# Two products accumulated in one PSUM bank, half of the activation read from it, and the last group's quarters stored one by one

## The chip, the cores and the metric

The kernel runs on one core of one Trainium2 chip. The core has five engines with queues of their own: TensorE (PE, matmuls; PEld is its weight load), VectorE (DVE), ScalarE (ACT), GpSimd (POOL) and SyncE (SP, which here only issues transfers). PE writes its results into PSUM, a small memory of eight banks of 512 fp32 columns on 128 partitions; DVE and ACT read PSUM, POOL does not. The metric is the device time in microseconds of one execution; lower is better.

## The reference

The input x has the shape 8 x 3008 x 256 (batch, sequence, features). First comes a two-dimensional Fourier transform over sequence and features of which the real part is kept; then each of the 24064 resulting rows goes through a two-layer network with 2048 hidden units and the activation h * sigmoid(1.702 h).

```python
X = np.fft.fft(x, axis=1)
X = np.fft.fft(X, axis=2)
attn = X.real.astype(np.float32).reshape(8 * 3008, 256)

h = attn @ w_in                              # 256 -> 2048
g = h * (1.0 / (1.0 + np.exp(-1.702 * h)))
out = (g @ w_out).astype(np.float32)         # 2048 -> 256
```

All is fp32.

## The kernel before, in words

**The transform.** 3008 = 94 x 32. For each batch element `fold1` (POOL) and `mix1` (PE, with a copy by ACT) do the part over 94, `spill` and `fill` turn the layout through DRAM, and `stage2` (PE, L277) does the part over 32. Its result is the tile pq, which holds two planes: P (`pq[:, 0]`) and Q (`pq[:, 1]`). The transform over the features is not carried out as such: it is folded into the first layer's weights (`fold_w`), which gives two weight tiles, `wcs[0]` for P and `wcs[1]` for Q. The first batch element has a faster way through the same stages (`mix_first`, `shuffle_first`), while the weights are still being loaded and rounded to fewer bits (`bounds`, `round_in`, `round_out`, `finish_in`, `finish_out`: lines L314 to L336, on ACT, POOL and DVE).

**The rows come in pairs.** Sequence rows s and -s have hidden values that are the sum and the difference of the product with P and the product with Q (with a correction of the Nyquist column, the tile nb times the scalar af2). So one pass over P and Q gives the hidden values of two rows.

**The steps.** Main work is a list of 384 steps (b, blk, hh, p): 8 batch elements, 3 blocks each, 2 halves hh of up to 256 columns (256, 241 or 240), and 8 pairs p of hidden chunks. The eight steps of one (b, blk, hh) form a group. In step t the code issues, one after the other:

- `hidden(t)`: four matmuls on PE. Two fill the bank pa with the product with P, two the bank pb with the product with Q (L397). ACT copies pa to the SBUF tile v (L401).
- `product(t - 3)`: the second layer for the step of three steps ago (L464). For the first group these are eight matmuls, for all later ones seven, in Strassen's scheme (the seven-product way to multiply 2 x 2 blocks), with sums of weights in wt and sums of activations in s. They add up over the eight steps of a group in the four PSUM tiles po0 to po3, which the pool holds once. At the group's end ACT copies po0's first half to u0 (L469).
- `activate(t - 1)` on ACT (L426), then the first two sums of `sums(t - 1)` on POOL (L438, L439), the other two of step t - 2 on DVE (L441, L442).
- `rows(t)` on DVE: h = v + pb (L411), then dif = nb * af2 - pb (L414, twice), then the mirrored rows h = v + dif (L421).
- `combine(t - 3)` on DVE, at a group's end only: the seven additions that undo Strassen's scheme (L493), each of which reads po, then two transposes (L495), then `store`, which issues 32 transfers (L512) for a half-block: on SP, or for the last group on SP and ACT by turns.
- what the schedule adds with `at(t, ...)`: `fold1` and `mix1` of the next batch element, `stage2`, the rounding of weights in the first steps.

Within an engine the order is that in which the code issues. Across engines only the data decide: an instruction waits for what it reads, and for those who still read what it overwrites. The pool `psm` has four PSUM banks for pa, pb and all transform stages, the pool `pso` the four banks of po.

```python
    for t in range(n + LAG):
        if t < n:
            hidden(t)
        if t >= LAG:
            product(t - LAG)
```

The functions that the diff touches, and what calls them:

Of the kernel before, what the change touches and what calls it, by code (L numbers as in the profile page):

```python
# [24 lines left out]
F32 = mybir.dt.float32  # L25
U32 = mybir.dt.uint32
ALU = mybir.AluOpType
ACTF = mybir.ActivationFunctionType
# [10 lines left out]
LAG = 3  # L39
# [6 lines left out]
def free(ap, offset, *dims):  # L46
    return bass.AP(ap.tensor, ap.offset + offset, [list(ap.ap[0])] + [list(d) for d in dims])
# [45 lines left out]
def kernel(ctx: ExitStack, tc, x, w_in, w_out, tab1, tab2, out):  # L93
    nc = tc.nc
    B, S, D = x.shape
# [3 lines left out]
    NBLK = NG // 4  # L99
# [7 lines left out]
    sp = ctx.enter_context(tc.tile_pool(name="sp", bufs=2, space=SB))  # L107
    op = ctx.enter_context(tc.tile_pool(name="op", bufs=2, space=SB))
# [10 lines left out]
    m2 = small[:, 0:256].rearrange("p (c n) -> p c n", c=2)  # L119
    rot = small[:, 256:384]  # L120
    cd = small[:, 384:384 + 4 * H].rearrange("p (i c d) -> p i c d", i=2, c=2)
    wcs = [const.tile([128, DF], F32, tag=f"wcs{i}", name=f"wcs{i}") for i in range(2)]
# [6 lines left out]
    def mat(w, j, rows=NA, n=96):  # L129
        return w[0:rows, j * 96:j * 96 + n]  # L130

    def bank(name):
        return psm.tile([128, 512], F32, tag="mm", name=name)
# [205 lines left out]
    last = {}  # L339
# [38 lines left out]
    steps = [(b, blk, hh, p) for b in range(B) for blk in range(NBLK) for hh in range(2) for p in range(NP)]  # L378
    vb, ht, st, pot, ot = {}, {}, {}, {}, {}

    def width(blk, hh):

        return 241 if (blk, hh) == (0, 1) else 240 if (blk, hh) == (NBLK - 1, 1) else 256

    def two(ap, n):
        return free(ap, 0, [256, 2], [1, n])

    def hidden(t):

        b, blk, hh, p = steps[t]  # L390
        n = width(blk, hh)
        pq, ks = pqt[b, blk], slice(hh * 256, hh * 256 + n)
        pa, pb = bank("pa"), bank("pb")
        for ps, cs in ((pa, 0), (pb, 1)):
            for i in range(2):
                f = 2 * p + i
                nc.tensor.matmul(ps[:, i * 256:i * 256 + n], lhsT=wcs[cs][:, f * 128:(f + 1) * 128],  # L397
                                 rhs=pq[:, cs, ks], start=True, stop=True)
        v = sp.tile([128, 512], F32, tag="v", name="v")

        nc.scalar.copy(two(v[:], n), two(pa[:], n))  # L401
        vb[t] = v, pb

    def rows(t):
        b, blk, hh, p = steps[t]
        n = width(blk, hh)
        nb, ks = nbt[b, blk], slice(hh * 256, hh * 256 + n)
        v, pb = vb.pop(t)
        h = ht[t] = hp.tile([128, 2, 2, 256], F32, tag="h", name="h")
        dif = sp.tile([128, 512], F32, tag="dif", name="dif")  # L410
        nc.vector.tensor_tensor(two(h[:], n), two(v[:], n), two(pb[:], n), op=ALU.add)  # L411
        for i in range(2):
            f = 2 * p + i
            nc.vector.scalar_tensor_tensor(dif[:, i * 256:i * 256 + n], nb[:, ks], af2[:, f:f + 1],  # L414
                                           pb[:, i * 256:i * 256 + n], op0=ALU.mult, op1=ALU.subtract)

        full, rest = divmod(n, NB)
        for at, blocks, m in ((0, full, NB), (full * NB, 1, rest)):
            if m:
                ins = [free(x[:], at, [256, 2], [NB, blocks], [1, m]) for x in (v, dif)]  # L420
                nc.vector.tensor_tensor(free(h[:], 512 + at + m - 1, [256, 2], [NB, blocks], [-1, m]), *ins, op=ALU.add)  # L421

    def activate(t):
        b, blk, hh, p = steps[t]
        g = free(ht[t][:], 0, [256, 4], [1, width(blk, hh)])
        nc.scalar.activation(g, g, ACTF.Gelu_apprx_sigmoid)  # L426

    def sums(t, eng):

# [11 lines left out]
            eng.tensor_tensor(s2, s1, a11, op=ALU.subtract)  # L441
            eng.tensor_tensor(s4, a12, s2, op=ALU.subtract)  # L442

    def product(t):

        b, blk, hh, p = steps[t]
        n = width(blk, hh)
        if p == 0:
            for q in range(4):
                pot[q] = pso.tile([128, 2, 256], F32, tag=f"o{q}", name=f"po{q}")  # L450
        h = ht.pop(t)
        if t < NP:

            plan = [(half, dh, wo[:, p, 2 * f + dh, :], h[:, half, f, :n], f)
                    for half in range(2) for dh in range(2) for f in range(2)]
        else:
            s = st.pop(t)
            plan = ((0, 0, wo[:, p, 0, :], h[:, 0, 0, :n], 0), (0, 1, wt[:, p, 1, :], s[:, 1, :n], 0),
                    (1, 0, wo[:, p, 2, :], h[:, 0, 1, :n], 0), (1, 1, wt[:, p, 2, :], s[:, 2, :n], 0),
                    (2, 0, wt[:, p, 0, :], s[:, 0, :n], 0), (2, 1, wo[:, p, 3, :], s[:, 3, :n], 0),  # L460
                    (3, 0, wt[:, p, 3, :], h[:, 1, 1, :n], 0))

        for q, i, lhs, rhs, f in plan:
            nc.tensor.matmul(pot[q][:, i, :n], lhsT=lhs, rhs=rhs, start=(p == 0 and i == 0 and f == 0),  # L464
                             stop=(p == NP - 1), skip_group_check=True)
        if p < NP - 1 or t < NP:
            return
        c1 = pot["c"] = op.tile([128, 256], F32, tag="u0", bufs=1, name="u0")
        nc.scalar.copy(c1[:, :n], pot[0][:, 0, :n])  # L469

    def combine(t):

        b, blk, hh, p = steps[t]
        if p < NP - 1:
            return
        n = width(blk, hh)
        o = op.tile([128, 4, 256], F32, tag="os", name="os")
        if t < NP:
            for half in range(2):
                nc.vector.transpose(o[:, 2 * half:2 * half + 2, :].rearrange("p i n -> p (i n)"),  # L480
                                    pot[half][:].rearrange("p i n -> p (i n)"))
        else:
            c = cv.tile([128, 4, 256], F32, tag="m", name="c")
            if n < 256:
                nc.gpsimd.memset(c[:, :, n:], 0.0)
            (_, m6), (m2, m7), (m5, m3), (m4, _) = ((pot[q][:, 0, :n], pot[q][:, 1, :n]) for q in range(4))
            u2, u3, u4 = (op.tile([128, 256], F32, tag=f"u{q}", bufs=1, name=f"u{q}")[:, :n] for q in (1, 2, 3))
            c1 = pot["c"][:, :n]
            c11, c12, c21, c22 = (c[:, q, :n] for q in range(4))
            for out_, i0, i1, how in ((u2, c1, m6, ALU.add), (c11, c1, m2, ALU.add), (u3, u2, m7, ALU.add),  # L490
                                      (u4, u2, m5, ALU.add), (c12, u4, m3, ALU.add), (c22, u3, m5, ALU.add),
                                      (c21, u3, m4, ALU.subtract)):
                nc.vector.tensor_tensor(out_, i0, i1, op=how)  # L493
            for half in range(2):
                nc.vector.transpose(*(x[:, 2 * half:2 * half + 2, :].rearrange("p i n -> p (i n)") for x in (o, c)))  # L495
        store(b, blk, hh, o, n)

    def store(b, blk, hh, o, n):

        a = 4 * blk + 2 * hh  # L500
        last = (b, blk, hh) == (B - 1, NBLK - 1, 1)
        for half in range(2):
            sign = -1 if half else 1
            row, step = sign * kp(0, a) % NA, sign * (kp(1, a) - kp(0, a))
            for i in range(8):
                dh, q = divmod(i, 4)
                src = o[32 * q:32 * q + 32, 2 * half + dh, :]
                eng = nc.scalar if last and i % 2 else nc.sync

                def put(row, k2s, places, src):  # L510
                    dst = view(out, (b * S + row) * D + 32 * i, [NA * D, k2s], [step * D, places], [1, 32])
                    eng.dma_start(out=dst, in_=src.rearrange("p (n c) -> p n c", c=32))  # L512

                full, rest = divmod(n, NB)
                put(row, NB, full, src[:, 0:full * NB])
                if rest:

                    k1, lo = kp(NU - 1, a + 1), rest - 16
                    k2, p0, p1 = (16 + lo, lo, 16) if half else (0, 0, rest)
                    put(k1 + NA * k2, p1 - p0, 1, src[p0:p1, 224:256])  # L520
# [57 lines left out]
    n = len(steps)  # L578
# [47 lines left out]

    for t in range(n + LAG):
        if t < n:
            hidden(t)
        if t >= LAG:  # L630
            product(t - LAG)
        if t in early:
            fold_w(early[t])
            nyquist_weights(early[t])

        if 0 < t <= n:
            activate(t - 1)
            sums(t - 1, nc.gpsimd)
        sums(t - 2, nc.vector)
        if t < n:  # L640
            rows(t)
        if t >= LAG:
            combine(t - LAG)
        for fn, args in extra.get(t, ()):
            fn(*args)
# [28 lines left out]
```

## Time and profile before

| | |
|---|---|
| time, median of 3 runs | 1973.1 us (1971.18 to 1975.15) |
| span of the profiled run | 1969.6 us |
| PE busy | 1938.4 us (98%) |
| DVE busy | 1555.3 us (79%) |
| POOL busy | 793.8 us (40%) |
| ACT busy | 695.8 us (35%) |
| L411, h = v + pb, DVE, 384 times | 675 ns each |
| L426, activation, ACT, 384 times | 1044 ns each |
| L401, copy of pa, ACT, 384 times | 577 ns each |
| matmuls L397 and L464 | 375 or 376 ns a record, two records a matmul |

An fp32 matmul shows as two records. Records overlap: a matmul of 256 columns takes 375 ns by its record, but two records start every 0.43 us. An engine's "busy" share is an average over the whole run; what matters is whether it is busy in the stretch in question, and who waits for it. In the lines of the order of time the columns are: start in us, duration in us (of all the instructions merged in the line), engine, line, operation, output <- inputs, shapes, how many, and in brackets the idle time before it and who ended it. In the table by stretch they are: stretch, its length, then busy time and number of instructions of PE, PEld, DVE, ACT and POOL, granted PE clock, share of the transfer engines, GB/s.

### The profile page before, as it was taken

What the parts mean: (1) busy time and instruction counts of PE and PEld (TensorE: products, weight loads), DVE (VectorE), ACT (ScalarE), POOL (GpSimd) and SP (SyncE); (2) the same over time, 40 slices, a digit from 0 to 9 for tenths busy, and PEclk for the clock granted to TensorE, in tenths of its full rate; (3) what the DMA queues carried; (4) which work ended last, traced back from release to release, by engine and by line L of the source; (5) the groups of instructions that cost most, each with busy time, mean ns of one, the idle gap of its engine ahead of it and who ended that gap; (6) DMA issues with size and microseconds to landing.
All of it is one profiled execution on the core that took longest, in us unless ns stands there. A gap on an engine that the chain in (4) does not pass through costs nothing.

```text
span 1969.6 us, 26665 instructions
## 1 busy us (share of the span) xinstructions
PE 1938.4 (98%) x9290; PEld 1724.3 (88%) x9290; DVE 1555.3 (79%) x2893; ACT 695.8 (35%) x970; POOL 793.8 (40%) x1065
## 2 busy tenths in 40 slices
PE   6999999999999999999999999999999999999997
PEld 4698899988989889888899888998899988989886
DVE  4778788888788777887788878887878888778776
ACT  2633333333333333333333333333333333333332
POOL 5476323543245332463325622255323543223232
PEclk8999999999999999999999999999999999999999
DMA  6720441216202252123422252221611213202201
GB/s 197 204 46 11 82 85 15 46 43 121 17 11 48 52 111 17 16 51 57 98 20 45 37 98 42 24 47 43 113 22 14 17 44 58 17 11 23 21 11 22
DMA packets 241837, 101.31 MB, mean 51 GB/s; under 512 B 209651, under 2 KB 232561, under 8 KB 239713
## 3 DMA queue, kind: packets, MB, share of 16 engines
q1 hardware_dynamic: 238965, 97.42, 28.7%
q10 hardware_dynamic: 2736, 2.18, 0.4%
q8 instruction: 73, 1.20, 0.3%
q14 instruction: 63, 0.52, 0.1%
HBM read 56.28 MB, written 45.76 MB: 52 GB/s over the span
## 4 chain that ended last, share of the span: by engine, by line
PE 96%; ACT 1%; DMA 1%; DVE 1%; issue 0%; POOL 0%; DVEq 0%; SPq 0%; POOLq 0%
PE po L464 58%; PE pa L397 16%; PE pb L397 16%; PE ps L189 2%; PE ps L277 2%; DMA raw<-in_moe_w_in_dram 0%; DMA t<-xt 0%; PE ps L241 0%; PE psw L366 0%; PE ps L240 0%; ACT g L314 0%; ACT r L322 0%; ACT r L321 0%; PE psa L372 0%; PE ps L192 0%
## 5 line engine op out<-in xcount | busy, mean ns | idle before, releaser
L438 POOL TENSOR_TENSOR s<-h 128x256 f32<-128x256 f32 (+2 forms) x376 | 273.8, 728 | 1098.2 <-ACT h L426 1026.6
L464 PE MATMUL po<-s,wt 128*128 128x256 f32 (+2 forms) x2256 | 600.0, 375 | 0.0
L401 ACT COPY v<-pa 128x512 f32<-128x512 f32 (+2 forms) x384 | 221.6, 577 | 893.1 <-PE pa L397 893.1
L411 DVE TENSOR_TENSOR h<-v,pb 128x512 f32<-128x512 f32 (+2 forms) x384 | 259.3, 675 | 336.6 <-PE pb L397 329.1
L464 PEld LDWEIGHTS po<-s,wt 128*128 128x128 f32 x2256 | 428.8, 190 | 48.3
L464 PE MATMUL po<-h,wo 128*128 128x256 f32 (+2 forms) x1632 | 469.9, 375 | 0.0
L421 DVE TENSOR_TENSOR h<-v,dif 128x512 f32<-128x512 f32 (+3 forms) x512 | 436.1, 871 | 13.2
L426 ACT ACTIVATE h<-h 128x1024 f32<-128x1024 f32 (+2 forms) x384 | 400.8, 1044 | 11.1 <-DVE h L421 11.1
L397 PE MATMUL pa<-pq,wcs 128*128 128x256 f32 (+2 forms) x1536 | 389.0, 376 | 0.0
L397 PE MATMUL pb<-pq,wcs 128*128 128x256 f32 (+2 forms) x1536 | 387.7, 375 | 0.0
L464 PEld LDWEIGHTS po<-h,wo 128*128 128x128 f32 x1632 | 310.1, 190 | 35.4
L414 DVE SCALAR_TENSOR_TENSOR dif<-nb,af,pb 128x256 f32<-128x256 f32 (+2 forms) x768 | 328.3, 469 | 0.0
L397 PEld LDWEIGHTS pb<-pq,wcs 128*128 128x128 f32 x1536 | 291.9, 190 | 33.0
L397 PEld LDWEIGHTS pa<-pq,wcs 128*128 128x128 f32 x1536 | 287.3, 190 | 33.0 <-issue 0.8
L439 POOL TENSOR_TENSOR s<-h 128x256 f32<-128x256 f32 (+2 forms) x376 | 277.6, 738 | 0.0
L442 DVE TENSOR_TENSOR s<-h,s 128x256 f32<-128x256 f32 (+2 forms) x376 | 211.3, 562 | 13.0
L464 PE MATMUL po<-h,wt 128*128 128x256 f32 (+2 forms) x752 | 220.5, 375 | 0.0
L464 PE MATMUL po<-s,wo 128*128 128x256 f32 (+2 forms) x752 | 220.5, 375 | 0.0
L441 DVE TENSOR_TENSOR s<-s,h 128x256 f32<-128x256 f32 (+2 forms) x376 | 175.3, 466 | 1.2 <-POOL s L438 1.2
L464 PEld LDWEIGHTS po<-s,wo 128*128 128x128 f32 x752 | 142.9, 190 | 16.1
L464 PEld LDWEIGHTS po<-h,wt 128*128 128x128 f32 x752 | 142.9, 190 | 16.1
L195 ACT COPY xt<-ps 96x512 f32<-96x512 f32 x56 | 32.5, 581 | 161.0 <-PE ps L189 151.2
(76 smaller groups left out, 878.0 us busy)
## 6 DMA issues: line engine op xcount, KB each, us to landing
out_dram<-os SPq DMA_DIRECT2D x512, 32.0 KB
Td<-xt SPq DMA_DIRECT2D x7, 1536.0 KB
t<-Td SPq DMA_DIRECT2D x7, 1536.0 KB
Xr<-in_x_dram SPq DMA_DIRECT2D x7, 1410.0 KB
xt<-in_x_dram SPq DMA_DIRECT2D x7, 1280.0 KB
xt<-Xr SPq DMA_DIRECT2D x7, 1200.0 KB
out_dram<-os SPq DMA_DIRECT2D x248, 28.0 KB
nb<-pq SPq DMA_DIRECT2D x23, 256.0 KB
```

Of the source, the lines that this page charges most:

```text
L189: nc.tensor.matmul(ps[0:96, o:o + D], lhsT=mat(w1, jj), rhs=t[:, NB - jj, :], start=True, stop=True)
L397: nc.tensor.matmul(ps[:, i * 256:i * 256 + n], lhsT=wcs[cs][:, f * 128:(f + 1) * 128], rhs=pq[:, cs, ks], start=True, stop=True)
L401: nc.scalar.copy(two(v[:], n), two(pa[:], n))
L411: nc.vector.tensor_tensor(two(h[:], n), two(v[:], n), two(pb[:], n), op=ALU.add)
L414: nc.vector.scalar_tensor_tensor(dif[:, i * 256:i * 256 + n], nb[:, ks], af2[:, f:f + 1], pb[:, i * 256:i * 256 + n], op0=ALU.mult, op1=AL ...
L421: nc.vector.tensor_tensor(free(h[:], 512 + at + m - 1, [256, 2], [NB, blocks], [-1, m]), *ins, op=ALU.add)
L426: nc.scalar.activation(g, g, ACTF.Gelu_apprx_sigmoid)
L438: eng.tensor_tensor(s1, a21, a22, op=ALU.add)
L439: eng.tensor_tensor(s3, a11, a21, op=ALU.subtract)
L441: eng.tensor_tensor(s2, s1, a11, op=ALU.subtract)
L442: eng.tensor_tensor(s4, a12, s2, op=ALU.subtract)
L464: nc.tensor.matmul(pot[q][:, i, :n], lhsT=lhs, rhs=rhs, start=(p == 0 and i == 0 and f == 0), stop=(p == NP - 1), skip_group_check=True)
```

## The change

There are three parts.

1. `hidden` is split in two. `hidden(t, 0)` computes the product with P into a bank pab, and ACT copies it to v, doubled (scale 2). `hidden(t, 1)` then adds the product with Q onto the same bank. The bank now holds P + Q, the hidden value of the first row, so L411 goes away; the mirrored row needs P - Q, which is 2P - (P + Q), so L414 and L421 do it with the doubled v and the same bank. `product` is split too, four matmuls and then the rest, and the order of issue becomes P, four matmuls of the older step, Q, the other three. This gives ACT's copy time to finish before PE writes the bank again.
2. `activate` works in two pieces: one on the mirrored rows in SBUF, one that reads P + Q from the bank and writes h.
3. In `combine` the additions are put in another order, and for the very last group each quarter of the result is transposed and stored as soon as it is there, its transfers alternating between SP and ACT.

The purpose is to take an addition per step off DVE, to use one PSUM bank a step and not two, and to begin the last stores sooner.

```diff
-    def hidden(t):
+    def hidden(t, cs):
...
-        pa, pb = bank("pa"), bank("pb")
-        for ps, cs in ((pa, 0), (pb, 1)):
-            for i in range(2):
-                f = 2 * p + i
-                nc.tensor.matmul(ps[:, i * 256:i * 256 + n], lhsT=wcs[cs][:, f * 128:(f + 1) * 128],
-                                 rhs=pq[:, cs, ks], start=True, stop=True)
-        v = sp.tile([128, 512], F32, tag="v", name="v")
-
-        nc.scalar.copy(two(v[:], n), two(pa[:], n))
-        vb[t] = v, pb
+        if cs == 0:
+            vb[t] = sp.tile([128, 512], F32, tag="v", name="v"), bank("pab")
+        v, ps = vb[t]
+        for i in range(2):
+            f = 2 * p + i
+            nc.tensor.matmul(ps[:, i * 256:i * 256 + n], lhsT=wcs[cs][:, f * 128:(f + 1) * 128], rhs=pq[:, cs, ks],
+                             start=(cs == 0 and i == 0), stop=(cs == 1), skip_group_check=True)
+        if cs == 0:
+
+            nc.scalar.activation(two(v[:], n), two(ps[:], n), ACTF.Copy, scale=2.0)
...
-        nc.vector.tensor_tensor(two(h[:], n), two(v[:], n), two(pb[:], n), op=ALU.add)
...
     def activate(t):
...
-        g = free(ht[t][:], 0, [256, 4], [1, width(blk, hh)])
+        n = width(blk, hh)
+        v, ps = vb.pop(t)
+        g = free(ht[t][:], 512, [256, 2], [1, n])
         nc.scalar.activation(g, g, ACTF.Gelu_apprx_sigmoid)
+        nc.scalar.activation(free(ht[t][:], 0, [256, 2], [1, n]), two(ps[:], n), ACTF.Gelu_apprx_sigmoid)
...
-        for q, i, lhs, rhs, f in plan:
+        for q, i, lhs, rhs, f in plan[4 * part:4 * part + 4]:
...
-            for out_, i0, i1, how in ((u2, c1, m6, ALU.add), (c11, c1, m2, ALU.add), (u3, u2, m7, ALU.add),
-                                      (u4, u2, m5, ALU.add), (c12, u4, m3, ALU.add), (c22, u3, m5, ALU.add),
+            for out_, i0, i1, how in ((c11, c1, m2, ALU.add), (u2, c1, m6, ALU.add), (u4, u2, m5, ALU.add),
+                                      (c12, u4, m3, ALU.add), (u3, u2, m7, ALU.add), (c22, u3, m5, ALU.add),
                                       (c21, u3, m4, ALU.subtract)):
                 nc.vector.tensor_tensor(out_, i0, i1, op=how)
+                if t < len(steps) - 1:
+                    continue
+                for q, done in enumerate((c11, c12, c21, c22)):
+                    if out_ is done:
+                        nc.vector.transpose(o[:, q, :], c[:, q, :])
+                        store(b, blk, hh, o, n, (q,))
...
-            hidden(t)
+            hidden(t, 0)
         if t >= LAG:
-            product(t - LAG)
+            product(t - LAG, 0)
+        if t < n:
+            hidden(t, 1)
+        if t >= LAG:
+            product(t - LAG, 1)
```

`rows` reads the bank under the name ps and no longer as pb; `store` takes the quarters to be stored as a further argument.

More of the change, by code (lines that the diff above doesn't have):

```diff
@@ L407, in rows @@
         nb, ks = nbt[b, blk], slice(hh * 256, hh * 256 + n)
-        v, pb = vb.pop(t)
+        v, ps = vb[t]
         h = ht[t] = hp.tile([128, 2, 2, 256], F32, tag="h", name="h")
         dif = sp.tile([128, 512], F32, tag="dif", name="dif")
-        nc.vector.tensor_tensor(two(h[:], n), two(v[:], n), two(pb[:], n), op=ALU.add)
         for i in range(2):
@@ L414, in rows @@
             nc.vector.scalar_tensor_tensor(dif[:, i * 256:i * 256 + n], nb[:, ks], af2[:, f:f + 1],
-                                           pb[:, i * 256:i * 256 + n], op0=ALU.mult, op1=ALU.subtract)
+                                           ps[:, i * 256:i * 256 + n], op0=ALU.mult, op1=ALU.subtract)
         full, rest = divmod(n, NB)
@@ L442, in sums, with product @@
             eng.tensor_tensor(s4, a12, s2, op=ALU.subtract)
-    def product(t):
+    def product(t, part):
         b, blk, hh, p = steps[t]
         n = width(blk, hh)
-        if p == 0:
+        if p == 0 and part == 0:
             for q in range(4):
                 pot[q] = pso.tile([128, 2, 256], F32, tag=f"o{q}", name=f"po{q}")
-        h = ht.pop(t)
+        h, s = ht[t], st.get(t)
         if t < NP:
@@ L456, in product @@
         else:
-            s = st.pop(t)
             plan = ((0, 0, wo[:, p, 0, :], h[:, 0, 0, :n], 0), (0, 1, wt[:, p, 1, :], s[:, 1, :n], 0),
@@ L461, in product @@
                     (3, 0, wt[:, p, 3, :], h[:, 1, 1, :n], 0))
-        for q, i, lhs, rhs, f in plan:
+        for q, i, lhs, rhs, f in plan[4 * part:4 * part + 4]:
             nc.tensor.matmul(pot[q][:, i, :n], lhsT=lhs, rhs=rhs, start=(p == 0 and i == 0 and f == 0),
                              stop=(p == NP - 1), skip_group_check=True)
+        if part == 0:
+            return
+        del ht[t]
+        st.pop(t, None)
         if p < NP - 1 or t < NP:
@@ L489, in combine @@
             c11, c12, c21, c22 = (c[:, q, :n] for q in range(4))
-            for out_, i0, i1, how in ((u2, c1, m6, ALU.add), (c11, c1, m2, ALU.add), (u3, u2, m7, ALU.add),
-                                      (u4, u2, m5, ALU.add), (c12, u4, m3, ALU.add), (c22, u3, m5, ALU.add),
+            for out_, i0, i1, how in ((c11, c1, m2, ALU.add), (u2, c1, m6, ALU.add), (u4, u2, m5, ALU.add),
+                                      (c12, u4, m3, ALU.add), (u3, u2, m7, ALU.add), (c22, u3, m5, ALU.add),
                                       (c21, u3, m4, ALU.subtract)):
                 nc.vector.tensor_tensor(out_, i0, i1, op=how)
+                if t < len(steps) - 1:
[4 more added lines that the diff above has]
+                        store(b, blk, hh, o, n, (q,))
+            if t == len(steps) - 1:
+                return
             for half in range(2):
@@ L496, in combine, with store @@
         store(b, blk, hh, o, n)
-    def store(b, blk, hh, o, n):
+    def store(b, blk, hh, o, n, part=(0, 1, 2, 3)):
         a = 4 * blk + 2 * hh
-        last = (b, blk, hh) == (B - 1, NBLK - 1, 1)
-        for half in range(2):
+        for half, dh in (divmod(x, 2) for x in part):
             sign = -1 if half else 1
             row, step = sign * kp(0, a) % NA, sign * (kp(1, a) - kp(0, a))
-            for i in range(8):
-                dh, q = divmod(i, 4)
+            for q in range(4):
+                i = 4 * dh + q
                 src = o[32 * q:32 * q + 32, 2 * half + dh, :]
-                eng = nc.scalar if last and i % 2 else nc.sync
+                eng = nc.scalar if len(part) == 1 and i % 2 else nc.sync
                 def put(row, k2s, places, src):
```

## The prediction, made before the changed kernel ran

> **What bounds the kernel now.** I read the first two parts of the page, then the busy time by stretch, then the order of time on TensorE (PE), VectorE (DVE) and ScalarE (ACT) in one steady step, in the ramp and at the end.
>
> ```profile
> PE 1938.4 (98%) x9290; PEld 1724.3 (88%) x9290; DVE 1555.3 (79%) x2893; ACT 695.8 (35%) x970; POOL 793.8 (40%) x1065
> PEclk8999999999999999999999999999999999999999
> ```
>
> ```profile
> 0.00:60.00 60.00, 44.03 (x148) 29.48 (x148) 25.80 (x30) 17.73 (x33) 30.09 (x26) 0.89 0.70 202
> 60.00:120.00 60.00, 57.08 (x259) 45.95 (x259) 50.00 (x66) 33.29 (x44) 33.83 (x29) 1.00 0.46 128
> 120.00:165.00 45.00, 45.00 (x226) 41.08 (x225) 38.36 (x65) 16.75 (x24) 29.85 (x44) 1.00 0.28 52
> 165.00:395.00 230.00, 230.00 (x1116) 206.16 (x1115) 186.31 (x346) 81.20 (x113) 97.55 (x133) 1.00 0.30 51
> 395.00:1940.00 1545.00, 1545.00 (x7465) 1385.76 (x7464) 1242.24 (x2364) 542.54 (x752) 597.98 (x830) 1.00 0.28 43
> 1940.00:1970.00 30.00, 17.32 (x86) 15.91 (x84) 12.58 (x27) 4.29 (x6) 4.51 (x7) 0.85 0.12 18
> ```
>
> The first number after each stretch's length is PE's busy time. From 120 to 1940 us PE is busy in every microsecond, at full clock. The 0.675 us of DVE work (L411) that the change saves in each of 384 steps therefore buys nothing by itself: PE has idle time only in the ramp (16 + 3 us) and in the tail (12.7 us). And whatever makes PE wait between 120 and 1940 is added to the time in full.
>
> **What the skill says.** The Trainium skill, "PSUM — Partial Sum Buffer", section "Engine vs sequencer instructions": ACT's and DVE's queues are strictly first in, first out, and matmuls start in program order. So one matmul waiting at the head of PE stops all behind it, and a copy in ACT's queue waits for all ahead of it; the ACT rows of the ramp below agree. The same page, rule 2 of "The four PSUM rules": a synchronised read of a partial sum in the middle of an accumulation is allowed. That makes the change legal, but no run yet shows its cost. "SBUF — State Buffer", section "SBUF: two separate sides": DVE and GpSimd (POOL) block each other only over a shared port, which a DVE operation with two SBUF inputs needs. The trace agrees: L421 (two SBUF inputs) takes 0.69 us alone and up to 2.69 us beside POOL, while L493 (one PSUM input) stays within 396 to 423 ns in all 329 cases.
>
> **Steady steps, parts that cost nothing.** The matmuls are the same in number and shape, and matmuls that accumulate (po) take 375 ns a record as those that don't (pa, pb), so PE's work is unchanged. DVE loses L411 (384 x 675 ns = 259 us): hidden behind PE. ACT's one activation of 1024 columns (1.044 us) becomes two of 512, each like the 0.577 us copy of 512 columns: some 0.1 us more a step on an engine that is 35% busy, hidden. PSUM banks: one a step instead of two.
>
> The new wait is that the matmuls with Q must wait for ACT's copy of P out of the same bank. A step in this stretch is 11 matmuls in 4.75 us (1182.33 to 1187.08), 0.431 us each:
>
> ```profile
> 1182.33 1.03 PE L397 MATMUL pa<-pq,wcs 128*128 128x256 f32 x4
> 1183.20 1.03 PE L397 MATMUL pb<-pq,wcs 128*128 128x256 f32 x4
> 1187.08 1.03 PE L397 MATMUL pa<-pq,wcs 128*128 128x256 f32 x4
> ```
> ```profile
> 1185.84 0.69 DVE L421 TENSOR_TENSOR h<-v,dif 128x512 f32<-128x512 f32 x1
> 1186.44 0.41 DVE L493 TENSOR_TENSOR u<-u,po 128x256 f32<-128x256 f32 x1
> 1186.78 0.41 DVE L493 TENSOR_TENSOR c<-u,po 128x256 f32<-128x256 f32 x1
> ```
>
> In the new order P ends at 0.86, four matmuls of the older step at 2.59, Q at 3.45, the rest at 4.75. The copy starts 0.25 us after P and takes 0.58, so it is done at 1.69, 0.9 us before PE asks for it. Cost nothing, hidden by the four matmuls between.
>
> **Steady steps, the part that costs.** What moves is the moment when DVE starts on a step. Today pb is ready at 1.73 us of the step, in the new order only at 3.45. From it: 0.27 us to DVE's start (in another step, pb's last matmul ends at 1130.04 and L411 starts at 1130.31), so 1185.79 to 1186.06 in this step's frame, 0.90 for the two L414, 0.61 for L421 to the next issue. `combine` stands behind it in DVE's queue and now starts at 1187.57, 0.49 us into the next step; before it started at 1186.44. It alone frees the four banks po, of which there is one set, for the next group's first product. And this product is now asked for after 0.86 us of the step instead of 1.73. The next group's p = 0 wants po0 at 1187.95. po0's last reader is u2, now second: 1187.90 to 1188.31, plus 0.05 to PE (as from the end of ACT's copy of wcs at 63.14 to psa at 63.19): PE waits 0.41. Then two matmuls to 1189.22; po1's last reader is u3, now fifth: two of the steps between are on the result just made (0.43 us apart, the others 0.33), so it starts at 1189.09 and ends at 1189.50: PE waits 0.33. po2 and po3 are free in time, since the second part comes after Q. Sum 0.74 us a group.
>
> Not each group pays. Where stage2 or mix1 (0.87 to 0.89 us of PE each) stands between combine and the next product, po0 is free in time. By the `at` calls, combine runs at t = 10, 18, 26, 34, 42, 50 of each batch element; t = 10, 26 and 42 have a stage2, 10 and 18 a mix1. Without either remain t = 34 (8 times), 50 (7), 18 in the first and last element (2) and 42 in the last (1): 18 groups x 0.74 = 13.3 us. The groups after 240 or 241 columns have a second L421 and lose some 0.2 us more in 5 or so places: 14 us in all. Nothing hides this, PE being the bound.
>
> **Ramp.** Steps 0 to 2 have no older product between P and Q, and up to step 5 ACT's queue holds the weight rounding (L314, L321, L322) ahead of the next step's copy. Today nobody on PE waits for that copy; then Q does.
>
> ```profile
> 65.76 1.06 ACT L426 ACTIVATE h<-h 128x1024 f32<-128x1024 f32 x1
> 66.72 1.15 ACT L314 ACTIVATE g<-raw 128x1024 f32<-128x1024 f32 x1
> 67.78 1.13 ACT L321 ACTIVATE r<-raw 128x1024 f32<-128x1024 uint32 x1
> 68.94 1.06 ACT L322 ACTIVATE r<-r 128x1024 uint32<-128x1024 f32 x1
> 69.91 0.57 ACT L401 COPY v<-pa 128x512 f32<-128x512 f32 x1
> ```
>
> This copy (step 2) ends at 70.48, while PE had done both its halves by 65.9. I walk the queues with these durations. Step 0: P to 55.57, copy to 56.80, Q 56.85 to 57.72: PE waits 1.3. Step 1: P to 58.58, copy behind the rounding to 60.48: 1.95. Then fold_w(1) to 64.87, its copies and psa to 66.65; the table load, gelu and rounding on ACT follow, and step 2's copy ends at 73.1 while its P was done at 67.6: 5.5. Step 3: product(0), first part, to 76.6, copy at 77.9: 1.4. fold_w(2) and psa to 85.9, product(1), first part, to 88.5, copy of step 4 behind gelu and rounding at 91.2: 2.7. From step 5 on the copy is in time. Waits 12.9; two waits of today (0.49 and 0.20) fall in them. PE at the end of product(3): 109.7 against 98.3 now, +11.4.
>
> One more thing: PE comes back slowly from a long wait. After the 5.2 us before 48.78, 16 records of L277 take 3.68 us; at full clock 8 take 1.05:
>
> ```profile
> 49.20 3.68 PE L277 MATMUL ps<-small,t 128*128 128x128 f32 x16
> 108.58 1.05 PE L277 MATMUL ps<-small,t 128*128 128x128 f32 x8
> ```
>
> After the 5.5 us of step 2 the same may come, mostly inside step 3's wait: +0.6. Ramp +12, between 8 (rounding finds less in its way) and 15.
>
> **Tail.** Now the two transposes end at 1959.6 and 16 stores a queue are issued from 1959.08, 0.49 us apart:
>
> ```profile
> 1959.08 7.82 ACTq L512 DMA_DIRECT2D out_dram<-os  x16
> ```
>
> The end follows 2.7 us after the last issue. By quarters, c11 (ready some 0.4 us after u1 at 1955.7) is transposed by 1956.5, so issuing starts 2.6 us earlier at the same pace; four issues a queue take 1.95 us, and the later quarters come every 1.2 to 1.4 us, so the queues never run dry. -2.6 us, between -1 and -3.5.
>
> **Sum.** 1973.1 + 14 + 12 - 2.6 = 1996.5 us.
>
> **Rivals.** (1) Only the ramp costs: combine starts earlier than I place it, or po is freed in time. For it: the margin is half a microsecond. Against: the order of DVE's queue is fixed, and the 0.27 us to its start is there in many steps. 1973.1 + 12 - 2.6 = 1982.5. (2) The copy of P, too, is late in many steps, since DVE's lag after a combine holds up gelu and so ACT's queue. For it: combine and transposes hold DVE for some 4 us. Against: by the walk gelu ends in the first half of a step and the 0.9 us of slack remain. With 0.3 us in the 56 steps that have a fold1 beside them, +17: 2013.5. (3) Not slower: the lighter DVE lets the ramp's rounding finish sooner, the waits fall in idle time that is there now, and the tail's gain stays: 1973.1 - 2.6 = 1970.5. For it: PE has 19 us of idle time in the ramp. Against: it lies before 54 us but for some 3 us.
>
> **Numbers.** Forecast 0.70; rival 1 0.13, rival 2 0.08, rival 3 0.09. The range goes from rival 1 (1982) to the forecast with po at 20 and ramp at 15: 1973.1 + 20 + 15 - 2.6 = 2005.5, so 2006. Slower is all but rival 3: 0.91; of rival 3 more than half ends within 0.2% (3.9 us).
>
> **What would show it.** PE idle before the first product matmuls of a group, released by DVE's combine, about 18 times 0.7 us; idle before the Q matmuls released by ACT's copy, in the first five steps only, some 13 us; DVE's combine starting half a microsecond into a step; the store issue beginning near 1956.5 in the old frame. Wrong if PE idles before Q in steady steps, if po's waits are absent, or if the span before 120 us is not some 12 us longer.

## The result and the profile after

| | before | after |
|---|---|---|
| time, median | 1972.7 us (1971.18 to 1975.15) | 2004.8 us (2004.05 to 2006.17) |
| ratio to before, 95% interval | | 1.0162 (1.0145 to 1.018) |
| span of the profiled run | 1969.6 us | 2003.1 us |
| DVE busy | 1555.3 us | 1223.7 us |

The changed kernel is 1.6% slower. 1996.5 was forecast, in a range up to 2006. The page of the changed kernel, parts 1 and 5:

```profile
PE 1956.9 (98%) x9290; PEld 1722.1 (86%) x9290; DVE 1223.7 (61%) x2511; ACT 720.1 (36%) x1354; POOL 780.1 (39%) x1065
...
L398 PE MATMUL pab<-pq,wcs 128*128 128x256 f32 (+2 forms) x3072 | 781.1, 377 | 9.2 <-ACT v L402 9.2
...
L467 PE MATMUL po<-h,wo 128*128 128x256 f32 (+2 forms) x1632 | 476.6, 378 | 8.8 <-DVE u L500 7.0
```

DVE gave up 332 us of work and the span grew by 33.5. The two idle columns name both new waits: Q (L398) for ACT's copy v, and the product (L467) for u2 and u3 of `combine`. They add up to only 18 us. The rest does not show as idle time. Matmuls at a lower clock, in the ramp, are busy time. And records overlap: in the order of time a matmul of 256 columns starts 0.43 us behind the one before it, but its two records last 0.59 us, so the first 0.16 us of each wait shows as busy. What PE really lost is read from starts alone: the next start, less the last one, less the number of records times 0.2157 us (for 256 columns; in proportion for fewer). A sum of such differences is good to some 0.5 us.

Where it went, by stretch (columns as in the table of before):

```profile
60.00:120.00 60.00, 49.95 (x193) 36.59 (x192) 33.61 (x39) 29.30 (x45) 26.70 (x19) 0.89 0.47 127
...
406.00:1970.00 1564.00, 1556.71 (x7470) 1382.06 (x7469) 967.14 (x2044) 563.75 (x1070) 589.02 (x832) 1.00 0.27 43
```

Between 60 and 120 us PE does 193 records where it did 259, at a mean clock of 0.89 and not 1.00. In the long stretch, which had no idle time at all, it now misses 7.3 us even by the busy measure. By starts the sum is this:

| stretch | lost, us | from |
|---|---|---|
| ramp, to the end of product(3) | 14.6 | 98.32 before, 112.96 after |
| steady steps | 21.2 | gaps between starts, to 1960 us: 21.8 after, 0.6 before |
| tail | -2.3 | the rest of 33.5 |

One group in the steady stretch, from the order of time on PE and DVE:

```profile
1211.44 0.87 DVE L414 SCALAR_TENSOR_TENSOR dif<-nb,af,pab 128x256 f32<-128x256 f32 x2 [2.36 <-PE pab L398]
...
1212.46 1.03 PE L398 MATMUL pab<-pq,wcs 128*128 128x256 f32 x4
1212.95 0.41 DVE L500 TENSOR_TENSOR c<-u,po 128x256 f32<-128x256 f32 x1
1213.28 0.94 DVE L500 TENSOR_TENSOR u<-u,po 128x256 f32<-128x256 f32 x2
...
1213.84 0.67 PE L467 MATMUL po<-h,wo 128*128 128x256 f32 x2 [0.35 <-DVE u L500]
...
1214.59 0.41 DVE L500 TENSOR_TENSOR u<-u,po 128x256 f32<-128x256 f32 x1
...
1215.06 0.70 PE L467 MATMUL po<-h,wo 128*128 128x256 f32 x2
```

P begins at 1212.46 and is over at 1213.32. DVE, which began the L414 of the step before at 1211.44, comes to `combine` at 1212.95, half a microsecond into the new step. PE starts on po0 at 1213.84, 0.15 us after u2 is done (0.52 us lost). It starts on po1 at 1215.06, 0.05 us after u3 (0.28 us lost). The bracket shows 0.35 us of the first wait and nothing of the second.

The ramp on ACT, and on PE:

```profile
71.97 0.58 ACT L430 ACTIVATE h<-pab 128x512 f32<-128x512 f32 x1
72.45 1.11 ACT L314 ACTIVATE g<-raw 128x1024 f32<-128x1024 f32 x1
73.45 1.12 ACT L321 ACTIVATE r<-raw 128x1024 f32<-128x1024 uint32 x1
74.60 1.06 ACT L322 ACTIVATE r<-r 128x1024 uint32<-128x1024 f32 x1
75.56 0.58 ACT L402 ACTIVATE v<-pab 128x512 f32<-128x512 f32 x1
```
```profile
63.11 5.10 PE L366 MATMUL psw<-wst,small 128*128 128x512 f32 x8
...
76.20 3.74 PE L398 MATMUL pab<-pq,wcs 128*128 128x256 f32 x8 [5.21 <-ACT v L402]
...
84.09 3.60 PE L366 MATMUL psw<-wst,small 128*128 128x512 f32 x8
```

Step 2's copy (75.56) stands behind the rounding, as foreseen, and Q waits 5.2 us. The same eight records of L366 take 5.10 us after the earlier waits and 3.60 later, and the eight records from 76.20 take 3.74 us where eight at full clock take 1.9.

PE's granted clock (the third number from the end) is at or near half of full speed in stretches that hold these slow records, and full from 80 us on:

```profile
57.00:60.00 3.00, 3.00 (x8) 2.29 (x8) 2.93 (x5) 2.86 (x3) 0.31 (x1) 0.50 0.78 208
...
63.00:66.00 3.00, 3.00 (x5) 1.36 (x5) 2.54 (x4) 0.00 (x0) 0.58 (x1) 0.50 0.52 138
...
76.00:80.00 4.00, 3.80 (x10) 3.03 (x11) 1.59 (x4) 3.97 (x6) 0.00 (x0) 0.53 0.95 311
80.00:84.00 4.00, 4.00 (x20) 3.54 (x19) 3.83 (x6) 0.75 (x2) 0.75 (x1) 1.00 1.15 411
```

The tail. DVE turns the first quarter, and both queues begin to issue:

```profile
1992.59 0.45 DVE L505 STREAM_TRANSPOSE os<-c 128x256 f32<-128x256 f32 x1
...
1993.07 7.88 ACTq L526 DMA_DIRECT2D out_dram<-os  x16
```

The last matmul starts near 1992.8 here and near 1957.0 before; the first store is issued at 1993.07 against 1959.08. Counted from the last matmul, the stores begin 1.9 us sooner and the span ends 2.3 us sooner (10.3 us behind it and not 12.7).

### The profile page after: what moved, and what is told of

The parts are those of the page before. It is cut to its first block, busy times and chain, and to the rows that moved or that the text cites. A ratio compares the mean times of both kernels' runs of the same rounds, so it can differ in the third digit from the quotient of the medians.

```text
span 2003.1 us, 27097 instructions
## 1 busy us (share of the span) xinstructions
PE 1956.9 (98%) x9290; PEld 1722.1 (86%) x9290; DVE 1223.7 (61%) x2511; ACT 720.1 (36%) x1354; POOL 780.1 (39%) x1065
## 4 chain that ended last, share of the span: by engine, by line
PE 93%; DVE 4%; DMA 1%; ACT 1%; issue 0%; POOL 0%; DVEq 0%; SPq 0%; POOLq 0%
PE po L467 55%; PE pab L398 32%; PE ps L189 2%; PE ps L277 2%; DVE u L500 1%; DVE dif L414 1%; DVE c L500 1%; DVE h L421 1%; PE psw L366 1%; DMA raw<-in_moe_w_in_dram 0%; DMA t<-xt 0%; PE ps L241 0%; PE ps L240 0%; DVE eu L227 0%; PE psa L372 0%
## 5 line engine op out<-in xcount | busy, mean ns | idle before, releaser
L398 PE MATMUL pab<-pq,wcs 128*128 128x256 f32 (+2 forms) x3072 | 781.1, 377 | 9.2 <-ACT v L402 9.2
L414 DVE SCALAR_TENSOR_TENSOR dif<-nb,af,pab 128x256 f32<-128x256 f32 (+2 forms) x768 | 330.0, 471 | 698.9 <-PE pab L398 682.9
L467 PE MATMUL po<-s,wt 128*128 128x256 f32 (+2 forms) x2256 | 660.7, 375 | 0.0
L398 PEld LDWEIGHTS pab<-pq,wcs 128*128 128x128 f32 x3072 | 581.4, 191 | 77.9 <-ACT v L402 11.1
L402 ACT ACTIVATE v<-pab 128x512 f32<-128x512 f32 (+2 forms) x384 | 226.2, 589 | 922.9 <-PE pab L398 922.9
L467 PE MATMUL po<-h,wo 128*128 128x256 f32 (+2 forms) x1632 | 476.6, 378 | 8.8 <-DVE u L500 7.0
L467 PEld LDWEIGHTS po<-s,wt 128*128 128x128 f32 x2256 | 428.6, 190 | 48.4
L467 PEld LDWEIGHTS po<-h,wo 128*128 128x128 f32 x1632 | 305.2, 190 | 61.8 <-DVE u L500 14.9
L421 DVE TENSOR_TENSOR h<-v,dif 128x512 f32<-128x512 f32 (+3 forms) x512 | 313.3, 632 | 13.2
L429 ACT ACTIVATE h<-h 128x512 f32<-128x512 f32 (+2 forms) x384 | 236.3, 615 | 6.2 <-DVE h L421 5.3
L446 DVE TENSOR_TENSOR s<-h,s 128x256 f32<-128x256 f32 (+2 forms) x376 | 219.4, 584 | 12.9
L430 ACT ACTIVATE h<-pab 128x512 f32<-128x512 f32 (+2 forms) x384 | 223.0, 581 | 0.0
L467 PE MATMUL po<-h,wt 128*128 128x256 f32 (+2 forms) x752 | 220.4, 375 | 0.0
L467 PE MATMUL po<-s,wo 128*128 128x256 f32 (+2 forms) x752 | 220.4, 375 | 0.0
L467 PEld LDWEIGHTS po<-h,wt 128*128 128x128 f32 x752 | 142.9, 190 | 16.1
L467 PEld LDWEIGHTS po<-s,wo 128*128 128x128 f32 x752 | 142.9, 190 | 16.1
L500 DVE TENSOR_TENSOR c<-u,po 128x256 f32<-128x256 f32 (+2 forms) x188 | 73.6, 411 | 7.2 <-PE po L467 4.0
L177 POOL TENSOR_TENSOR xt<-xt 94x510 f32<-94x510 f32 (+1 forms) x56 | 69.0, 1233 | 4.4
```

The source lines that it names most:

```text
L402: nc.scalar.activation(two(v[:], n), two(ps[:], n), ACTF.Copy, scale=2.0)
L430: nc.scalar.activation(free(ht[t][:], 0, [256, 2], [1, n]), two(ps[:], n), ACTF.Gelu_apprx_sigmoid)
```

## The experiments

Every run carries its own runs of the kernel before on the same chip (1972.6 to 1972.8 us). For the ramp the traces also give a figure of their own, the time from the first P of step 0 to that of step 7: 43.7 us in the kernel before, 58.4 in the changed kernel. It leaves out the lead-in, whose length differs from trace to trace: in the traces of the kernels that leave it as it was, step 0 starts between 54.2 and 57.5 us.

**Does the tail pay by itself?** The kernel before, with the changed kernel's additions and stores by quarters for the last group alone; the other groups keep the old order.

```diff
+                for q, done in enumerate((c11, c12, c21, c22)):
+                    if out_ is done:
+                        nc.vector.transpose(o[:, q, :], c[:, q, :])
+                        store(b, blk, hh, o, n, (q,))
```

> The kernel before with only the last group's quarters turned and stored one by one. My theory: the tail is bound by the issue of 16 stores a queue, so it ends 2.3 us sooner (what the trace of the changed kernel leaves for the tail): about 0.12% faster, 1970.4 beside 1972.7. Rival, that the tail is bound by the last additions and the landing of the last store: no change, within 0.3 us.

Measured: 1970.8 us, 0.9991 of before (0.9984 to 0.9997). The tail's part is real, 1.9 us, and it is the change's only gain.

**Is it `combine` that PE waits for?** The changed kernel, with the additions of all groups but the last in the order of before.

```diff
+            if t < len(steps) - 1:
+                quarters = ((u2, c1, m6, ALU.add), (c11, c1, m2, ALU.add), (u3, u2, m7, ALU.add),
+                            (u4, u2, m5, ALU.add), (c12, u4, m3, ALU.add), (c22, u3, m5, ALU.add),
+                            (c21, u3, m4, ALU.subtract))
```

> The changed kernel with combine's additions in the order of the kernel before (u2, c11, u3, u4, ...) for all groups but the last. My theory, PE waits for po0 and po1 behind combine in DVE's queue: po0 comes free 0.33 us sooner, po1 0.86 us sooner, so of the 0.98 us a group (0.55 for po0, 0.25 for po1, 0.18 of slow restart) 0.3 to 0.45 stays; 10 to 12 us faster than the changed kernel, about 1993.5. Rival, that PE's new idle time comes from the weight loads or from the matmul with Q and not from combine: no change, 2004.8.

Measured: 1988.0 us, 1.0076 (1.0063 to 1.0089), so 16.8 us less than the changed kernel and more than was expected. By starts, 5.1 us of the 21.8 are left: 0.10 to 0.17 us for po0 and 0.1 of restart behind it, and nothing for po1. Another order of five additions in DVE's queue takes away three quarters of the steady loss.

**Does an earlier Q do the same?** Three matmuls between P and Q and not four:

```diff
-        for q, i, lhs, rhs, f in plan[4 * part:4 * part + 4]:
+        for q, i, lhs, rhs, f in plan[3 * part:3 + 5 * part]:
```

> The changed kernel with three matmuls of the older step between P and Q and not four. My theory: Q ends 0.43 us sooner, so DVE and its combine start 0.43 us sooner; po0 is then free just in time, but po1 is asked for before Q and still waits about 0.25 to 0.3 us in 18 groups. 10 to 12 us faster than the changed kernel, about 1993.5; the copy of P still has 0.4 us to spare, so no wait before Q in steady steps. Rival, that Q is held by ACT's copy in steady steps: slower, by 0.1 us a step or more, 2040.

Measured: 1995.8 us, 1.0116 (1.01 to 1.0131), 9.0 us less than the changed kernel. By starts 11.8 us of waits are left. po1 keeps its 0.23 to 0.29 us in nearly every one of the 18 groups, as expected. po0 was expected just in time and still waits 0.11 to 0.20 us. No wait before Q appears in the steady steps.

**Is it the order of issue or the shared bank?** The kernel before with only the order P, four matmuls, Q, three matmuls; P and Q keep banks of their own and DVE keeps its addition.

```diff
-            hidden(t)
+            hidden(t, 0)
         if t >= LAG:
-            product(t - LAG)
+            product(t - LAG, 0)
+        if t < n:
+            hidden(t, 1)
+        if t >= LAG:
+            product(t - LAG, 1)
```

> The kernel before with only the new order of issue (P, four matmuls of the older step, Q, the other three); P and Q keep their own banks and DVE its addition. My theory, it is the order that makes DVE late and po's next use early, not the shared bank: DVE starts 0.1 us before the changed kernel's start of a step but has 0.6 us more to do, so combine starts 1.1 us into the next step and, with u2 first, po0 is free at 1.6 us against 0.86 asked for: about 0.9 us in 18 groups, a little in others; 16 to 20 us slower than before, 1990, and no loss in the ramp, where Q waits for no copy. Rival, that the waits come from sharing the bank: the same as before, 1972.7.

Measured: 1989.4 us, 1.008 (1.0063 to 1.0097). In the order of time of this kernel, P (here L399 on pa) is again followed by a wait:

```profile
483.06 1.03 PE L399 MATMUL pa<-pq,wcs 128*128 128x256 f32 x4
...
484.15 0.41 DVE L496 TENSOR_TENSOR u<-u,po 128x256 f32<-128x256 f32 x1
...
484.62 0.70 PE L463 MATMUL po<-h,wo 128*128 128x256 f32 x2 [0.53 <-DVE u L496]
```

0.70 us are lost in this group, 16.5 in all. The split alone makes a steady loss, without any shared bank, and here even with u2 as the first addition: `combine` begins at 484.15, 1.1 us into the step, because DVE still has the 0.69 us of L411 to do. po_order has the same split and the same order of additions, but no L411, and loses 5.1. So the lighter DVE, worth nothing where PE never waits for DVE, goes with some 11 us less once the split makes PE wait; the two kernels also differ in the shared bank and the two-piece activation, so that L411 alone makes this difference was not tried.

**What does the split buy?** The changed kernel with P, Q, then all seven matmuls.

> The changed kernel with P and Q issued one behind the other, then all seven matmuls of the older step. My theory: each Q then waits for ACT's copy in full (0.25 us to its start, 0.6 us of copy, 0.15 us to PE), about 1.0 us in each of 384 steps, so some 380 us slower, while DVE gets Q 0.7 us sooner in a step and the po waits go: about 2365. Rival, that PE takes up later work while Q waits: 2005 or less.

Measured: 2373.4 us, 1.2032 (1.201 to 1.2054). On PE, every step now looks like this:

```profile
1500.38 0.97 PE L398 MATMUL pab<-pq,wcs 128*128 128x240 f32 x4
1502.07 1.08 PE L398 MATMUL pab<-pq,wcs 128*128 128x240 f32 x4 [0.72 <-ACT v L402]
```

Four records of 240 columns take 0.81 us, so Q starts 0.88 us late, and some 0.1 us more follows at the next matmul. With one bank for P and Q, work in between is a must. The change chose enough of it, and more than enough.

**Are the two waits on po independent?** Two buffers for po0, which takes one bank from the other stages.

```diff
-    psm = ctx.enter_context(tc.tile_pool(name="psm", bufs=4, space=PS))
+    psm = ctx.enter_context(tc.tile_pool(name="psm", bufs=3, space=PS))
...
-                pot[q] = pso.tile([128, 2, 256], F32, tag=f"o{q}", name=f"po{q}")
+                pot[q] = pso.tile([128, 2, 256], F32, tag=f"o{q}", bufs=2 if q == 0 else 1, name=f"po{q}")
```

> The changed kernel with two PSUM buffers for po0 (one bank fewer for the others, three and not four). My theory: the first wait (0.55 us, for po0) goes, but po1 is then asked for 0.55 us sooner and comes free no sooner, so the second wait grows from 0.25 to 0.8 us: the sum of waits falls only by one slow restart, 0.1 us in 18 groups; 2003, between 2001 and 2005. Rival, that the two waits are independent: 11 us faster, 1994.

Measured: 2010.2 us, 1.0191 (1.0177 to 1.0205). The total missed: it is slower than the changed kernel, since with three banks the ramp has new waits (the second half of L366 waits 0.68 us for ACT's copy of the first, and others behind it). The steady part did as its theory said, short of the 0.1 us a group that was to be gained:

```profile
502.13 0.59 PE L467 MATMUL po<-h,wo 128*128 128x256 f32 x2
502.56 0.59 PE L467 MATMUL po<-s,wt 128*128 128x256 f32 x2
...
503.86 0.70 PE L467 MATMUL po<-h,wo 128*128 128x256 f32 x2 [0.71 <-DVE u L500]
```

po0 starts at once, and po1 then loses 0.87 us where the two lost 0.52 and 0.28. With the restarts it is 0.98 us a group in both kernels. From step 7 to step 383 this kernel takes 21.8 us more than the kernel before, the changed kernel 21.2. What binds is the time at which DVE gets through `combine`, not either bank.

**The ramp: is it Q behind the copy?** A bank of its own for Q, and the addition on DVE, in steps 0 to 6.

```diff
+        elif t < RAMP:
+            vb[t] = vb[t][0], bank("pb")
...
+        if t < RAMP:
+            nc.vector.tensor_tensor(two(h[:], n), two(v[:], n), two(ps[:], n), op=ALU.add)
```

> The changed kernel with a bank of its own for Q, and the addition on DVE, in steps 0 to 6 as in the kernel before. My theory: the whole 14.6 us that the ramp lost (9.2 us of waits before Q, some 5 us of matmuls at a lower clock behind them) come back: 1990. Rival, that the ramp lost its time to the two-piece activation and the order of issue: at most 5 us come back, 2000 or more.

Measured: 1991.6 us, 1.0089 (1.0074 to 1.0104), 13.3 us less than the changed kernel. From 60 to 120 us PE is busy for 57.2 us again, at a clock of 1.00. Steps 0 to 6 take 43.8 us, as in the kernel before (43.7): by the traces the whole 14.6 us come back.

**Is it the rounding ahead of the copy?** `bounds` of step t is issued in step t + 1, behind that step's copy of P.

```diff
+        for fn, args in extra.get(t - 1, ()):
+            if fn is bounds:
+                fn(*args)
         if t >= LAG:
             product(t - LAG, 0)
```

> The changed kernel with the rounding's ACT work of each early step (bounds) issued one step later, behind that step's copy of P. My theory, the copy stands behind the rounding in ACT's queue: the waits before Q fall from 9.2 to about 5 us (what is left is the copy itself and, in step 2, table load and activation), and with fewer microseconds at a low clock some 5 us come back: 2000. Rival, that Q waits for the copy whatever ACT has to do: 2004.8.

Measured: 2000.2 us, 1.0135 (1.012 to 1.015), 4.6 us less; steps 0 to 6 take 52.9 us and not 58.4. Step 2's wait falls from 5.2 to 2.1 us, and step 4's, 2.1 before, is gone; those of steps 0 and 1 stay at 1.1 and 0.7. So part of the ramp is the rounding, the rest is that Q waits for a copy at all.

**Does the clock cost anything of its own?** Nine matmuls on constant data in the waits between P and Q.

```diff
+        if t in FILL:
+            warm(FILL[t])
...
+    FILL = {0: 1, 1: 1, 2: 5, 4: 2}
```

> The changed kernel with nine matmuls on constant data (128x512, as the kernel's warm-up uses) between P and Q of steps 0, 1, 2 and 4, one, one, five and two. They do no useful work; they only fill the wait for ACT's copy. My theory, some 5 us of the ramp's 14.6 are matmuls at a low clock after the waits: 3 to 5 us faster than the changed kernel although it has 8 us more of matmuls, 2001. Rival, no cost of the clock: the same or up to 2 us slower, 2004.8 to 2007.

Measured: 2003.2 us, 1.0148 (1.0133 to 1.0164), 1.7 us less than the changed kernel, with intervals that overlap, and less than the 3 to 5 expected, though 60 to 120 us now run at a clock of 1.00 throughout. The traces say it more surely: steps 0 to 6 take 55.3 us and not 58.4, so 3.2 us less although nine matmuls were added. The slow matmuls cost time of their own. But of some 6 us at a low clock (worked out below) only about half comes back; new waits for the copy stand in steps 2 and 3 (1.0 and 0.9 us).

**All parts mended.** The order of additions, three matmuls before Q, and banks of their own in steps 0 to 6, with the last quarters stored one by one.

> The changed kernel with both of these edits, and with a bank of their own for Q (and the addition on DVE) in steps 0 to 6 as in the kernel before. My theory: the 21.2 us of waits on po and the 14.6 us of the ramp both go, the 2.3 us of the tail stay: 1970.4, the same as the kernel before with the tail alone, for PE is the bound and the lighter DVE gives nothing. Rival, that a lighter DVE shortens the steady stretch as soon as nothing else stands in the way: below 1965.

Measured: 1969.9 us, 0.9984 (0.9978 to 0.9991). The stretch that lost 21 us:

```profile
125.00:1940.00 1815.00, 1815.00 (x8776) 1627.36 (x8774) 1165.92 (x2396) 663.28 (x1257) 712.71 (x1001) 1.00 0.28 45
```

PE is busy in all of it, and DVE has 304 us less work than in the kernel before (1251.3 against 1555.3). The time is that of the tail alone: 1969.9 beside 1970.8 on the same chip, with intervals that overlap. The traces put the steady steps side by side more sharply. From the first P of step 7 to that of step 383 it takes 1845.87 us here (102.43 to 1948.30), in the kernel before (98.32 to 1944.19) and in tail_only (101.22 to 1947.09). The losses of the changed kernel are accounted for, and a lighter DVE buys nothing that can be measured.

**Two more ideas on top.** Five matmuls on constant data where PE waits for a transfer before L268; and then the last stores on SP, ACT and POOL by turns.

```diff
     nyquist_weights(0)
+    warm(5)
     rotate(0, 0, 4, nc.scalar.copy)
...
+                eng = (nc.sync, nc.scalar, nc.gpsimd)[i % 3] if len(part) == 1 else nc.sync
```

> The kernel of all_three with five matmuls on constant data between nyquist_weights(0) and rotate(0), where PE waits 5.2 us for a transfer in each of the kernels. My theory: PE then keeps its full clock, and the 16 records of L277 behind it take 1.8 and not 3.6 us, as do some after them; 2 us faster than all_three, 1968. Rival, that ACT's copies set the pace there: as all_three, 1969.9.

> The same, with the last group's 32 stores issued from SP, ACT and POOL by turns. My theory: the tail is bound by the issue of stores, 0.49 us each on a queue; some 11 a queue and not 16 would end it up to 2 us sooner, but the last quarter is ready 1.9 us after half of the issuing, so 1 to 1.5 us faster than without POOL, 1966.8. Rival, that POOL's issue or landing is slower than the other two: no gain or a loss of up to 2 us.

Measured: 1968.6 us, 0.9979 (0.9972 to 0.9986), and 1968.6 us, 0.998 (0.9971 to 0.9988). In the first, the 16 records of L277 take this:

```profile
50.72 2.03 PE L277 MATMUL ps<-small,t 128*128 128x128 f32 x16
```

instead of 3.68 us in the kernel before. That the whole is faster than all_three by 1.3 us lies within the intervals. POOL as a third queue gave nothing: it took 8 of the 32 stores and the other two 12 each, so the issue ended sooner (after 6.5 us, not 7.7), but from the first store to the end of the span it took 9.5 us against 9.6. So with three queues the tail is no longer bound by the issue; by what, was not settled.

## Why the prediction was right, point by point

- **PE is the bound, and the lighter DVE is worth nothing by itself.** Right, shown by all_three. DVE lost 332 us of work and not 259, since L421 also became shorter (871 ns in the mean before, 632 after); that too bought nothing.
- **Activation in two pieces, the copy in steady steps: nothing.** Right for the time: no wait before Q after the ramp, in the changed kernel or with three matmuls between.
- **Waits on po, 14 us.** Right in mechanism and place, shown by po_order, split_only and po0_two. The 18 groups are there, and `combine` starts 0.49 us into the step as worked out. The size was off, 21.2 us, and three terms of the sum made it so. po0 cost 0.52 to 0.57 us and not 0.41. In the group shown u2 is done 1.23 us into the step, exactly as worked out; it is the way from u2's end to PE's start that took 0.15 us and not 0.05. po1 cost 0.23 to 0.28 (once 0.34) and not 0.33. A term was missing: after each wait the next matmul is late as well, by 0.07 to 0.11 us. That is 17.7 us in the 18 groups, where I had 13.3. The other groups were taken for free, but for 5 or so with 240 or 241 columns; 23 groups in which stage2 or mix1 stands between lose 0.08 to 0.43 us each, some 3.5 us together.
- **Ramp, 12 us.** Right in mechanism, shown by ramp_two_banks and, in part, by late_round; 14.6 by the trace. Here the split into terms was wrong in both ways. The waits were 9.2 us and not 12.9: 1.1, 0.7, 5.2, 0 and 2.1 where I had 1.3, 1.95, 5.5, 1.4 and 2.7. The low clock, for which I had 0.6 us, made up the difference and more: by starts, some 6 us, in three stretches of slow matmuls, two of them behind waits of about a microsecond. I had counted it for the longest wait alone. So that the ramp came out near 12 is in part luck: the waits were put nearly 4 us too high and the clock some 5 us too low. The walk is also loose in itself: its waits less the two of the kernel before give 12.2 us, its end point 11.4.
- **Tail, -2.6 us.** -2.3 by the trace, -1.9 as a part by itself. The stores begin 1.9 us sooner, not 2.6. The reason given, that the issue of the stores is the bound, holds for two queues only as far as fixed_warm_pool shows: with three, it is not.
- **Rivals.** Rival 1, only the ramp: what it left out is 21 us. Rival 2, a late copy in many steps: absent. Rival 3, hidden in the ramp's idle time: that time lies earlier, and the ramp lost all.

## What to carry to other kernels

When one engine is busy without a gap, work taken off another is worth nothing as long as the busy engine doesn't wait for it, and every new dependency of the busy engine is to be priced first. Moving an instruction later on the busy engine moves all that hangs on it: here Q went back by four matmuls, so DVE's in-order queue reached the additions that free the next group's banks half a microsecond after they were asked for. An order of instructions (c11 before u2) can become worth 17 us when there is no slack. In the kernel before there is slack: in the group of the prediction's lines, u2 is done at 1186.85 and po0 is asked for at 1188.81. That the new order would be harmless there follows from these times; no run tried it.

## What was not expected of the hardware

- A wait on PE costs more than its length. After the 0.55 us for po0 the next matmul starts 0.08 us late, after the 0.25 us for po1 0.10 us, in all 18 groups. The weight load shows as waiting too (PEld in front of L467 for u of L500, 14.9 us in 40 cases), so here it did not run ahead through the wait. In the group shown, po1's first weight load and its matmul start together, at 1215.06; the next record follows 0.32 us later, where two records without a wait are 0.22 us apart.
- In the ramp PE's clock fell near waits of only a microsecond: behind 1.1 us of waiting, at 56.78, eight records took 3.78 us and not 1.9. The length of the wait alone does not decide: 2.1 us of waiting before 94.33, in the same trace, left the clock at 1.00, as did half a microsecond 18 times in the steady stretch and 0.98 and 0.93 us in ramp_filled, where matmuls on constant data fill the rest of the waits. (PE had also waited 5.2 us at 43.6 and had just come back to full clock; that the earlier wait plays a part was not tried.)
